# Pair transposes, sums from the pair's sum, a ScalarE read for a drain, and a new order of all queues, in a gated linear attention with a maxout layer behind it

## Chip, cores, metric

One core of a Trainium2 chip. The metric is the device time of one execution in microseconds (us), as the median of several runs. All text below says TensorE (PE, weight loads PEld), VectorE (DVE), ScalarE (ACT), GpSimd (POOL) and SyncE (SP).

## The reference

```python
# q, k, v, f_logit: (4, 8, 768, 48) float32
f = 1.0 / (1.0 + np.exp(-f_logit))
for t in range(S):
    state = f[:, :, t, :, None] * state + np.einsum('bhd,bhe->bhde', k[:, :, t], v[:, :, t])
    y[:, :, t] = np.einsum('bhd,bhde->bhe', q[:, :, t], state)
x = y.transpose(0, 2, 1, 3).reshape(B * S, H * D)      # 3072 x 384
out = np.maximum(x @ w1, x @ w2) @ w_out               # d_ff 1024
```

The kernel cuts the sequence into chunks and works through 12 steps (three windows of 256 positions for each of four batches). It uses max(a, b) = relu(a - b) + b: with wd = w1 - w2 and m2 = w2 w_out, the layer is relu(x wd) w_out + x m2.

## The kernel before

A list of words sets the order in which instructions enter each engine's queue; a number behind a letter is the step. The words that matter here: E (exponential and logarithm), C (sums over positions, on TensorE), X (exponentials of the sums), K and Q (scaled k and q), V (cast of v), T (transposes), A (scores), S (part of y that comes from the state), Y (part of y from the values, then y to SBUF), D and N (state update), d (h pieces), o (o pieces), and w words for the weights. These parts are touched (cut; `...` marks cuts):

```python
def stage_E(s):                                   # ScalarE
    nc.scalar.activation(flat(tmp), flat(loaded[s]["f"]), AF.Exp, bias=0.0, scale=-1.0)
    nc.scalar.activation(pad("ell", s)[:, :, :, 0:D], by_parity(tmp), AF.Ln, bias=1.0, scale=1.0)

def stage_C(s):                                   # 4 matmuls of 384 columns, 8 of 2
    ...
    for pt in range(2):
        for par in range(2):
            nc.tensor.matmul(out=..., lhsT=u_str if par > pt else u_inc,
                             rhs=ell[:, par, :, 0:D], start=(par == 0), stop=(par == 1))
    for j in range(NP):
        for par in range(2):
            nc.tensor.matmul(out=..., lhsT=ell[:, par, 2*j:2*j+2, :]..., rhs=ones2, ...)

def stage_T(s):                                   # 64 transposes in 64x64 tiles
    for x, nm in enumerate(("kp", "qp")):
        for j in range(NP):
            for par in range(2):
                for r in range(2):
                    for h in range(2):
                        nc.tensor.transpose(out=ps[h][r*DP:(r+1)*DP, x, j, par, :],
                            in_=src[rows, par, 2*j + r, :], identity=ident[rows, rows])

def stage_Yv(s):
    mark()                                        # nc.tensor.drain().then_inc(s_sem, 1)
    nc.tensor.wait_ge(s_sem, s_tick[s])           # S has to be in PSUM before Y adds to it
    for j ... for par ... for r ... for h in range(2):
        nc.tensor.matmul(out=ys[s][h]..., lhsT=vb[...], rhs=m[...], ...)
```

## Time and profile before

| | before |
|---|---|
| time, median of the first runs | 165.42 us (165.03 to 168.61) |
| span of the profiled execution (167.49 us) | 165.6 us |
| first h piece starts (end of the start) | 38.95 us |
| first h piece to the start of the last o piece's second part ("the middle") | 121.1 us |
| TensorE instructions | 5564 |

The two rows on the start and the middle come from TensorE's timeline. This profile is of a slow execution: 167.49 us, 2 us above the median here. So differences of start and middle to it can be too large by as much; the times and ratios are the measure.

### The profile page before, as it was taken

The page shows a single profiled execution, that of the slowest core. Times are in us where ns is not written, and L with a number is a line of the kernel's source. Part 1 is how long each engine was busy: PE and PEld are TensorE (multiplying, and loading weights), DVE is VectorE, ACT ScalarE, POOL GpSimd, SP SyncE. Part 2 cuts the span into 40 slices and gives each one's busy share as a digit, 9 for nine tenths or more (in the row PEclk, how much of TensorE's full clock was granted, in tenths as well). Part 3 has the DMA queues.
Part 4 walks back from the last instruction along what each step waited for, and adds up shares of the span by engine and source line. Part 5 has one row for each costly group of instructions (what it writes and reads, how often), then busy time and mean ns, then how long its engine had stood idle before and what let it go on. Part 6 is the DMA issues. An engine that isn't in the chain of part 4 may idle for free.

```text
span 165.6 us, 6262 instructions
## 1 busy us (share of the span) xinstructions
PE 137.5 (83%) x2780; PEld 97.4 (59%) x2781; DVE 102.8 (62%) x178; ACT 86.4 (52%) x166; POOL 46.0 (28%) x51
## 2 busy tenths in 40 slices
PE   0339839999999689999479998979985999999990
PEld 0226725557867466866347666757754776778650
DVE  6947799658659949898507729576979136201121
ACT  3568325479994966959222962717122723454400
POOL 7341611040633504390000985115410001000000
PEclk9999985899999999999978999999999999999999
DMA  5999999999999999985968096100153002202004
GB/s 137 261 304 358 331 337 363 231 276 262 265 252 258 242 272 260 299 236 144 275 177 192 4 251 194 50 16 0 53 155 113 4 0 105 101 16 95 4 22 168
DMA packets 55132, 29.32 MB, mean 177 GB/s; under 512 B 50624, under 2 KB 52800, under 8 KB 55104
## 3 DMA queue, kind: packets, MB, share of 16 engines
q1 hardware_dynamic: 53568, 28.32, 65.9%
q10 hardware_dynamic: 1536, 0.59, 1.5%
q8 instruction: 22, 0.36, 1.0%
q14 instruction: 6, 0.05, 0.1%
HBM read 23.59 MB, written 4.72 MB: 171 GB/s over the span
## 4 chain that ended last, share of the span: by engine, by line
PEld 34%; issue 21%; PE 12%; DMA 12%; PEldq 5%; SPq 5%; DVE 4%; POOL 3%; ACT 1%; ACTq 1%; POOLq 0%; DVEq 0%
PEld L363 12%; PEld L376 6%; DMA xT<-xT 6%; DMA kt<-in_k_dram 5%; PEldq L270 5%; PE o L376 5%; SPq L92 4%; PEld L232 3%; PE h L363 3%; PEld L249 3%; PEld L309 2%; PEld L373 2%; PE o L373 2%; PE y L309 2%; POOL qp L215 2%
## 5 line engine op out<-in xcount | busy, mean ns | idle before, releaser
L365 ACT ACTIVATE gT<-h 128x512 bf16<-128x512 f32 x48 | 27.7, 607 | 31.3 <-PE h L363 27.7
L363 PE MATMUL h<-xT,wd 128*128 128x256 bf16 x288 | 35.4, 273 | 5.3 <-issue 3.3
L376 PE MATMUL o<-wo,gT 128*128 128x384 bf16 x192 | 36.4, 335 | 0.3 <-issue 0.3
L378 DVE COPY ob<-o 128x384 f32<-128x384 f32 x24 | 13.2, 553 | 36.9 <-PE o L376 36.8
L261 DVE TENSOR_TENSOR at_m<-at,mask 128x512 bf16<-128x512 f32 x48 | 29.8, 681 | 5.8 <-PE at L249 5.8
L363 PEld LDWEIGHTS <-wd 128*128 128x128 bf16 x288 | 27.0, 98 | 10.0 <-issue 5.7
L340 POOL TENSOR_TENSOR state<-tmp_s,f_last 128x256 bf16<-128x256 f32 x16 | 11.6, 730 | 61.1 <-DVE tmp_s L339 55.4
L376 PEld LDWEIGHTS <-gT 128*128 128x128 bf16 x192 | 19.1, 100 | 13.8 <-issue 1.9
L215 POOL TENSOR_TENSOR kp<-kt,f_inv 128x768 bf16<-128x768 f32 x9 | 16.3, 1814 | 25.0 <-ACT f_inv L208 19.9
L347 ACT CAST xT<-y 128x512 bf16<-128x512 f32 x24 | 12.9, 588 | 12.7 <-PE y L309 12.5
L236 DVE COPY trs<-trp 128x1024 bf16<-128x1024 bf16 x24 | 15.4, 683 | 2.2 <-PE trp L232 1.8
L190 PE MATMUL cum<-ell,u_inc 128*128 128x384 bf16 x36 | 10.8, 358 | 6.3 <-ACT ell L181 6.2
L373 PE MATMUL o<-m,xT 128*128 128x384 bf16 x72 | 15.9, 330 | 0.0
L208 ACT ACTIVATE f_inv<-cum 128x384 f32<-128x384 f32 x24 | 10.4, 487 | 8.0 <-PE cum L197 5.6
L180 ACT ACTIVATE tmp_e<-ft 128x768 f32<-128x768 f32 x12 | 10.4, 868 | 4.8 <-DMA ft<-in_f_logit_dram 3.0
L249 PE MATMUL at<-trs 48*64 48x128 bf16 x384 | 9.6, 236 | 3.3 <-DVE trs L236 2.0
L215 POOL TENSOR_TENSOR qp<-qt,f_dec 128x768 bf16<-128x768 f32 x6 | 11.9, 1986 | 0.0
L219 DVE CAST vb<-vt 128x768 bf16<-128x768 f32 x12 | 11.2, 933 | 1.0 <-DMA vt<-in_v_dram 1.0
L208 ACT ACTIVATE f_dec<-cum 128x384 f32<-128x384 f32 x24 | 10.6, 505 | 0.0
L309 PE MATMUL y<-at_m,vb 64*64 64x128 bf16 x384 | 8.9, 226 | 1.7 <-PEq L270 0.6
L181 ACT ACTIVATE ell<-tmp_e 128x768 bf16<-128x768 f32 x12 | 10.1, 843 | 0.4
L249 PEld LDWEIGHTS <-trs 48*64 48x64 bf16 x384 | 7.2, 118 | 5.3 <-issue 2.8
(60 smaller groups left out, 149.3 us busy)
## 6 DMA issues: line engine op xcount, KB each, us to landing
ft<-in_f_logit_dram SPq DMA_DIRECT2D x12, 384.0 KB, 6.3
vt<-in_v_dram SPq DMA_DIRECT2D x12, 384.0 KB, 6.4
kt<-in_k_dram SPq DMA_DIRECT2D x12, 384.0 KB, 6.3
qt<-in_q_dram SPq DMA_DIRECT2D x12, 384.0 KB, 6.2
out_dram<-ob SPq DMA_DIRECT2D x12, 384.0 KB, 3.1
w_f<-in_moe_w_dram SPq DMA_DIRECT2D x6, 512.0 KB, 7.4
wo_f<-in_moe_w_out_dram SPq DMA_DIRECT2D x2, 768.0 KB, 9.4
xT<-xT ACTq DMA_DIRECT2D x24, 24.0 KB, 3.4
```

What stands on the lines that cost most here:

```text
L208: nc.scalar.activation(t[:, pt, :], ps[pt][:, 0:HD], AF.Exp, bias=0.0, scale=scale)
L215: engine.tensor_mul(pad(nm + "p", s)[:, :, :, 0:D], by_parity(loaded[s][nm]), t.rearrange("p two (h d) -> p two h d", h=H))
L236: nc.vector.tensor_copy(t[:, h], ps[h])
L249: nc.tensor.matmul(out=ps[r][h * HC:(h + 1) * HC, j % 2, par, :], lhsT=t[rows, h, 0, j, par, :], rhs=t[rows, h, 1, j].rearrange("p a t -> ...
L261: nc.vector.tensor_mul(m[:, r, 2 * jj:2 * jj + 2], ps[r], mask.rearrange("p j a b t -> p j a (b t)"))
L309: nc.tensor.matmul(out=ys[s][h][r * DP:(r + 1) * DP, j, :], lhsT=vb[rows, par, 2 * j + r, :], rhs=m[rows, r, j, par, :], start=first, stop ...
L347: nc.scalar.copy(x[:, :, :, h, :], ps.rearrange("p j (a t) -> p j a t", a=2))
L363: nc.tensor.matmul(out=ps[:, f, :], lhsT=wd[:, kt, ff * C:(ff + 1) * C], rhs=xT[g][:, kt, :], start=(kt == 0), stop=(kt == KT - 1))
L365: nc.scalar.activation(gT[g][:, 2 * fp:2 * fp + 2, :], ps, AF.Relu)
L373: nc.tensor.matmul(out=ps, lhsT=xT[g][:, kt, cols], rhs=m2[:, kt, :], start=(kt == 0), stop=False)
L376: nc.tensor.matmul(out=ps, lhsT=gT[g][:, ff, cols], rhs=wo[:, ff, :], start=False, stop=(ff == FG - 1))
L378: nc.vector.tensor_copy(obs[g][:, par, :], ps)
```

## The change

Intent: fewer TensorE instructions (transposes by pairs, sums of both positions of a pair formed beforehand), no drain of TensorE between S and Y, and a new order of every queue to fit. The new list does more than reorder: among other things it moves three scalings of k and two of the three weight subtractions from VectorE to GpSimd, two casts of wd from ScalarE to VectorE and one cast of v from VectorE to ScalarE, and it loads the weights part by part. "The new order" below means all of this. Core of the diff (abridged; order lists, the removed lines of stage C and helpers for single weight parts left out):

```diff
 def stage_E(s):
-    nc.scalar.activation(pad("ell", s)[:, :, :, 0:D], by_parity(tmp), AF.Ln, bias=1.0, scale=1.0)
+    nc.scalar.activation(flat(both), flat(both), AF.Ln, bias=1.0, scale=1.0)
+    nc.scalar.copy(even, both[:, :, 0, :])
+def stage_e(s, engine):                       # GpSimd for words e, VectorE for words g
+    engine.tensor_add(pad("es", s)[:, :, 0:D], both[:, :, 0, :], both[:, :, 1, :])
 def stage_C(s):
+    nc.tensor.matmul(out=outs[0], lhsT=ident, rhs=even, start=True, stop=False)
+    nc.tensor.matmul(out=outs[0], lhsT=u_str, rhs=es[:, :, 0:D], start=False, stop=True)
+    nc.tensor.matmul(out=outs[1], lhsT=u_inc, rhs=es[:, :, 0:D], start=True, stop=True)
+    for j in range(NP): nc.tensor.matmul(out=..., lhsT=es[:, 2*j:2*j+2, :]..., rhs=ones2, ...)
 def stage_T(s):
-    for r in range(2):
-        for h in range(2):
-            nc.tensor.transpose(out=ps[h][r*DP:(r+1)*DP, x, j, par, :], in_=src[rows, par, 2*j+r, :], ...)
+    for h in range(2):
+        pair = src[rows, par, 2*j:2*j+2, :].rearrange("p r d -> p (r d)")
+        nc.tensor.transpose(out=ps[h][:, x, j, par, :], in_=pair, identity=ident[rows, rows])
+def stage_Z(s):                               # placed by its own word in the order
+    nc.scalar.copy(seen, ys[s][1][:, :, 0])   # Y's first matmul into this bank waits for the read
 def stage_Yv(s):
-    mark()
-    nc.tensor.wait_ge(s_sem, s_tick[s])
-    ... for h in range(2):
+    ... for h in (1, 0):
```

More of the change, by code (lines that the diff above doesn't have):

```diff
@@ L17 @@
 ORDER = """
-P Lf:0 Lv:0 Lf:1 Lk:0 Lq:0 E0 V0 C0 Lq:1 X0 W2 q0 E1 K0 Lk:1 Lv:1 T0 C1 Wo wca0 wcp2 D0 A0 Lf:2 N0
-W1 X1 Lf:3 S0 k1 V1 Lk:2 Lf:4 wca1 Y0 Lq:2 wT0 wT1 Q1 wT2 wop1 woa0 Lv:2 D1 Lk:3 woa3 T1 E2 N1 wov2
-Lv:3 Lv:4 A1 S1 wm0 wm2 Lq:3 ws0 Y1 ws1 Lf:5 C2 wm1 ws2 wd11v Lv:5 X2 wd00v wm5 Lq:4 wm4 Lq:5 E3 wm3
-Lk:4 wd10v Lf:6 wd02a wd12v Lf:7 wd01a Lk:5 C3 K2 Lf:8 Lv:6 q2 X3 V2 d0.0 T2 D2 E4 d0.1 d0.2 d0.3 V3
-Lf:9 Lk:6 N2 d1.0 d1.1 A2 d1.2 d1.3 K3 C4 o0.0 Q3 T3 X4 Lq:6 S2 V4 E5 Y2 D3 N3 A3 Lq:7 C5 Lk:7 Lk:8
@@ L23 @@
-q4 o0.1 X5 o1.0 K4 E7 T4 Lf:10 Lv:7 E6 d2.0 Lq:8 S3 Y3 A4 q5 V5 C6 o1.1 X6 Lk:9 d2.1 Lk:10 K5 K6 T5
-C7 X7 d2.2 d2.3 E8 D4 q6 D5 Lq:9 d3.0 Q7 V6 N4 N5 d3.1 d3.2 k7 S4 Y4 A5 o2.0 Lv:8 C8 E9 V7 X8 d3.3
-o2.1 T7 Lk:11 S5 Y5 T6 d4.0 d4.1 Lq:10 o3.0 A6 D6 d4.2 K8 Q8 N6 d4.3 V8 Lf:11 C9 o3.1 X9 E11 S6 E10
-D7 Y6 o4.0 d5.0 N7 Lv:9 K9 Lv:10 o4.1 A7 T8 Q9 d5.1 C11 V9 X11 d5.2 d5.3 d6.0 D8 T9 S7 Y7 Lq:11 D9
-A8 k11 o5.0 d6.1 C10 X10 q10 d6.2 V10 K10 d6.3 o5.1 d7.0 Q11 o6.0 T10 Lv:11 S8 Y8 D10 A9 V11 o6.1 S9
@@ L28 @@
-Y9 A10 T11 d7.1 d7.2 d7.3 d8.0 d8.1 o7.0 d8.2 o7.1 d8.3 A11 S10 D11 Y10 d9.0 o8.0 o8.1 d9.1 d9.2
-d9.3 S11 Y11 d10.0 d10.1 o9.0 o9.1 d10.2 d10.3 d11.0 d11.1 d11.2 d11.3 o10.0 o11.0 o11.1 o10.1
+Lf:0 W2:2 E0 Lk:0 wca2 W2:0 P Lf:1 e0 Lv:0 wca0 Lq:0 C0 Wo:0 X0 K0 E1 V0 wT0 D0 Lf:2 g1 N0 wov1 W2:1
+Wo:1 E2 q0 Lk:1 T0 wcp1 C1 g2 Lq:1 Lv:1 X1 woa3 A0 S0 W1:1 Z0 Lf:3 wT1 C2 W1:2 wov0 K1 X2 W1:0 Lk:2
+q1 wT2 wop2 Y0 T1 Lq:2 V1 wm0 E3 wsp1 Lf:4 A1 wm1 D1 Lv:2 wsp2 K2 wm2 g3 S1 Lq:3 Lf:5 Q2 wsv0 N1
+Lk:3 C3 Z1 Lv:3 X3 Y1 E4 wd02v Q3 wd00v wd01v Lq:4 wd12v wd10v Lk:4 Lf:6 wd11v T2 Lv:4 Lk:5 d0.0 e4
@@ new lines @@
+d0.1 d0.2 V2 Lf:7 A2 D2 K3 Lq:5 Lv:5 E5 d0.3 wm5 wm3 d1.0 d1.1 N2 wm4 d1.2 C4 S2 V3 Z2 Lf:8 X4 Q4 T3
+D3 Lv:6 g5 N3 Lq:6 Y2 d1.3 A3 C5 V4 K4 X5 o0.0 E6 o0.1 D4 Lf:9 S3 Z3 T4 Lq:7 Lk:6 Lv:7 N4 q5 Lf:10
+E7 Y3 d2.0 g7 o1.0 A4 d2.1 K5 Lk:7 d2.2 e6 Lk:8 C7 Lq:8 Lv:8 T5 X7 C6 Lf:11 X6 E8 V5 e8 o1.1 A5 Q6
+S4 Z4 d2.3 d3.0 D5 Y4 d3.1 Lq:9 N5 V6 o2.0 K6 Lk:9 S5 Z5 E9 o2.1 e9 Y5 T6 K7 d3.2 d3.3 d4.0 d4.1 q7
+A6 Lv:9 Lv:10 C8 X8 K8 d4.2 d4.3 C9 Lk:10 X9 T7 D6 V8 V7 N6 E11 o3.0 e11 q8 E10 o3.1 o4.0 e10 D8 D7
@@ L30 @@
+S6 N7 A7 Z6 Y6 o4.1 d5.0 V9 d5.1 d5.2 d5.3 S7 T8 Z7 K9 Y7 d6.0 Q9 C11 X11 d6.1 Lq:10 o5.0 d6.2 Lk:11
+d6.3 T9 A8 S8 Lq:11 Z8 o5.1 V10 Lv:11 d7.0 o6.0 Y8 D9 o6.1 K11 d7.1 A9 C10 Q11 X10 S9 Z9 q10 d7.2
+d7.3 d8.0 K10 Y9 T10 o7.0 D10 A10 d8.1 o7.1 U11 d8.2 d8.3 S10 T11 Z10 Y10 D11 o8.0 o8.1 d9.0 A11 S11
+d9.1 d9.2 Z11 d9.3 d10.0 d10.1 Y11 o9.0 d10.2 d10.3 o9.1 o10.0 d11.0 d11.1 d11.2 d11.3 o10.1 o11.0
+o11.1
 """
@@ L97, with load_rows, load_wo @@
     wo_f = wst.tile([C, FG, HD], F32, name="wo_f")
-    def load_rows(dst, w):
-        for kt in range(KT):
-            nc.sync.dma_start(out=dst[:, kt, :], in_=w[kt * C:(kt + 1) * C, :])
-    def load_wo():
-        for h in range(2):
-            part = slice(h * FG // 2, (h + 1) * FG // 2)
-            nc.sync.dma_start(out=wo_f[:, part, :],
-                              in_=moe_w_out.rearrange("(j p) m -> p j m", p=C)[:, part, :])
+    def load_rows(dst, w, kt):
+        nc.sync.dma_start(out=dst[:, kt, :], in_=w[kt * C:(kt + 1) * C, :])
+    def load_wo(h):
+        part = slice(h * FG // 2, (h + 1) * FG // 2)
+        nc.sync.dma_start(out=wo_f[:, part, :],
+                          in_=moe_w_out.rearrange("(j p) m -> p j m", p=C)[:, part, :])
     tri = consts.tile([C, 2, HC], BF16, name="tri")
@@ L127 @@
     padded = {}
-    for nm, n_bufs in (("ell", 2), ("kp", 3), ("qp", 2), ("vb", 3)):
+    for nm, n_bufs in (("es", 2), ("kp", 3), ("qp", 2), ("vb", 3)):
         padded[nm] = []
         for i in range(n_bufs):
-            t = consts.tile([C, 2, H, DP], BF16, name=f"{nm}{i}")
+            t = consts.tile([C, H, DP] if nm == "es" else [C, 2, H, DP], BF16, name=f"{nm}{i}")
             nc.vector.memset(t, 0.0)
@@ L176, in by_parity @@
         return t.rearrange("p h two d -> p two h d")
+    ell = {}
     def stage_E(s):
-        tmp = work.tile([C, H, 2, D], F32, name="tmp_e", tag="tmp_e", bufs=1)
-        nc.scalar.activation(flat(tmp), flat(loaded[s]["f"]), AF.Exp, bias=0.0, scale=-1.0)
-        nc.scalar.activation(pad("ell", s)[:, :, :, 0:D], by_parity(tmp), AF.Ln, bias=1.0,
-                             scale=1.0)
-    def stage_C(s):
-        ell = pad("ell", s)
-        cum[s] = []
-        for pt in range(2):
-            ps = bank("cum")
-            for par in range(2):
-                nc.tensor.matmul(out=ps[:, 0:HD].rearrange("p (h d) -> p h d", h=H),
-                                 lhsT=u_str if par > pt else u_inc, rhs=ell[:, par, :, 0:D],
-                                 start=(par == 0), stop=(par == 1))
-            cum[s].append(ps)
-        ps = cum[s][0]
+        both = work.tile([C, H, 2, D], F32, name="both", tag="both")
+        even = work.tile([C, H, D], BF16, name="even", tag="even")
+        nc.scalar.activation(flat(both), flat(loaded[s]["f"]), AF.Exp, bias=0.0, scale=-1.0)
+        nc.scalar.activation(flat(both), flat(both), AF.Ln, bias=1.0, scale=1.0)
+        nc.scalar.copy(even, both[:, :, 0, :])
+        ell[s] = (both, even)
@@ new lines, in stage_e @@
+    def stage_e(s, engine):
+        both = ell[s][0]
+        engine.tensor_add(pad("es", s)[:, :, 0:D], both[:, :, 0, :], both[:, :, 1, :])
+    def stage_C(s):
+        even, es = ell.pop(s)[1], pad("es", s)
+        cum[s] = [bank("cum") for _ in range(2)]
+        outs = [ps[:, 0:HD].rearrange("p (h d) -> p h d", h=H) for ps in cum[s]]
+        nc.tensor.matmul(out=outs[0], lhsT=ident, rhs=even, start=True, stop=False)
+        nc.tensor.matmul(out=outs[0], lhsT=u_str, rhs=es[:, :, 0:D], start=False, stop=True)
+        nc.tensor.matmul(out=outs[1], lhsT=u_inc, rhs=es[:, :, 0:D], start=True, stop=True)
@@ L195, in stage_C @@
         for j in range(NP):
-            for par in range(2):
-                nc.tensor.matmul(out=ps[:, HD + 2 * j:HD + 2 * j + 2],
-                                 lhsT=ell[:, par, 2 * j:2 * j + 2, :].rearrange("p h e -> p (h e)"),
-                                 rhs=ones2, start=(par == 0), stop=(par == 1))
+            nc.tensor.matmul(out=cum[s][0][:, HD + 2 * j:HD + 2 * j + 2],
+                             lhsT=es[:, 2 * j:2 * j + 2, :].rearrange("p h e -> p (h e)"),
+                             rhs=ones2, start=True, stop=True)
@@ L216, in stage_M, with stage_V @@
                           t.rearrange("p two (h d) -> p two h d", h=H))
-    def stage_V(s):
-        nc.vector.tensor_copy(pad("vb", s)[:, :, :, 0:D], by_parity(loaded[s]["v"]))
+    def stage_V(s, copy):
+        copy(pad("vb", s)[:, :, :, 0:D], by_parity(loaded[s]["v"]))
     def stage_T(s):
@@ L228, in stage_T @@
                 for par in range(2):
-                    for r in range(2):
-                        for h in range(2):
-                            rows = slice(h * HC, (h + 1) * HC)
-                            nc.tensor.transpose(out=ps[h][r * DP:(r + 1) * DP, x, j, par, :],
-                                                in_=src[rows, par, 2 * j + r, :],
-                                                identity=ident[rows, rows])
+                    for h in range(2):
+                        rows = slice(h * HC, (h + 1) * HC)
+                        pair = src[rows, par, 2 * j:2 * j + 2, :].rearrange("p r d -> p (r d)")
+                        nc.tensor.transpose(out=ps[h][:, x, j, par, :], in_=pair,
+                                            identity=ident[rows, rows])
         for h in range(2):
@@ L249, in stage_A @@
                             nc.tensor.matmul(out=ps[r][h * HC:(h + 1) * HC, j % 2, par, :],
-                                             lhsT=t[rows, h, 0, j, par, :],
-                                             rhs=t[rows, h, 1, j].rearrange("p a t -> p (a t)"),
-                                             start=True, stop=True, skip_group_check=True)
+                                                  lhsT=t[rows, h, 0, j, par, :],
+                                                  rhs=t[rows, h, 1, j].rearrange("p a t -> p (a t)"),
+                                                  start=True, stop=True, skip_group_check=True)
             at[s, jj] = ps
@@ L262, in stage_A_dve @@
                                      mask.rearrange("p j a b t -> p j a (b t)"))
-    ys, s_tick, s_open = {}, {}, []
-    s_sem = tc.alloc_semaphore("s_done")
-    def mark():
-        if s_open:
-            nc.tensor.drain().then_inc(s_sem, 1)
-            s_tick[s_open.pop()] = len(s_tick) + 1
+    ys = {}
     def has_state(s, h):
@@ L293, in stage_S @@
                         start=(j == 0), stop=False, skip_group_check=True)
-                    s_open[:] = [s]
+    def stage_Z(s):
+        seen = work.tile([C, NP], F32, name="seen", tag="seen")
+        nc.scalar.copy(seen, ys[s][1][:, :, 0])
     def stage_Yv(s):
         m, vb = at.pop(s), pad("vb", s)
-        mark()
-        if s in s_tick:
-            nc.tensor.wait_ge(s_sem, s_tick[s])
         for j in range(NP):
@@ L305, in stage_Yv @@
                 for r in range(2):
-                    for h in range(2):
+                    for h in (1, 0):
                         rows = slice(h * HC, (h + 1) * HC)
@@ L363, in piece_d @@
                 nc.tensor.matmul(out=ps[:, f, :], lhsT=wd[:, kt, ff * C:(ff + 1) * C],
-                                 rhs=xT[g][:, kt, :], start=(kt == 0), stop=(kt == KT - 1))
+                                      rhs=xT[g][:, kt, :], start=(kt == 0), stop=(kt == KT - 1))
         nc.scalar.activation(gT[g][:, 2 * fp:2 * fp + 2, :], ps, AF.Relu)
@@ L373, in piece_o @@
             nc.tensor.matmul(out=ps, lhsT=xT[g][:, kt, cols], rhs=m2[:, kt, :],
-                             start=(kt == 0), stop=False)
+                                  start=(kt == 0), stop=False)
         for ff in range(FG):
@@ L417, with subtract @@
     wdn = []
-    def subtract(kt):
+    def subtract(kt, engine):
         if not wdn:
             wdn.append(wst.tile([C, KT, d_ff], BF16, name="wdn", tag="w_b"))
-        nc.vector.tensor_sub(wdn[0][:, kt, :], w1_f[:, kt, :], w2_f[:, kt, :])
+        engine.tensor_sub(wdn[0][:, kt, :], w1_f[:, kt, :], w2_f[:, kt, :])
     def wd_permuted(h, i, copy):
@@ L436, in rows_of @@
     def rows_of(dst, w):
-        return lambda a: load_rows(dst, w)
+        return lambda a: load_rows(dst, w, int(a))
     steps = {
@@ L441 @@
         "Lq": lambda a: load("q", int(a)), "Lv": lambda a: load("v", int(a)),
-        "W1": rows_of(w1_f, moe_w1), "W2": rows_of(w2_f, moe_w2), "Wo": lambda a: load_wo(),
-        "E": attention(stage_E), "C": attention(stage_C), "X": attention(stage_X),
+        "W1": rows_of(w1_f, moe_w1), "W2": rows_of(w2_f, moe_w2), "Wo": attention(load_wo),
+        "E": attention(stage_E), "e": lambda a: stage_e(int(a), nc.gpsimd),
+        "g": lambda a: stage_e(int(a), nc.vector), "C": attention(stage_C), "X": attention(stage_X),
         "K": lambda a: stage_M(int(a), "k", nc.gpsimd), "k": lambda a: stage_M(int(a), "k", nc.vector),
         "Q": lambda a: stage_M(int(a), "q", nc.gpsimd), "q": lambda a: stage_M(int(a), "q", nc.vector),
-        "V": attention(stage_V), "T": attention(stage_T), "S": attention(stage_S),
+        "V": lambda a: stage_V(int(a), nc.vector.tensor_copy), "U": lambda a: stage_V(int(a), nc.scalar.copy),
+        "T": attention(stage_T), "S": attention(stage_S), "Z": attention(stage_Z),
         "A": lambda a: (stage_A(int(a)), stage_A_dve(int(a))),
@@ L455 @@
         "wm": lambda a: m2_natural(int(a)) if int(a) < KT else m2_permuted(int(a) - KT),
-        "ws": attention(subtract), "wd": lambda a: wd_permuted(int(a[0]), int(a[1]), copies[a[2]]),
+        "ws": lambda a: subtract(int(a[1]), nc.vector if a[0] == "v" else nc.gpsimd), "wd": lambda a: wd_permuted(int(a[0]), int(a[1]), copies[a[2]]),
     }
```

## The prediction

> **What bounds the kernel now.** I read the busy shares first, then the slices, the chain of waits, and last TensorE's own timeline, because the first three do not say why TensorE loses time. From the page:
>
> ```profile
> span 165.6 us, 6262 instructions
> PE 137.5 (83%) x2780; PEld 97.4 (59%) x2781; DVE 102.8 (62%) x178; ACT 86.4 (52%) x166; POOL 46.0 (28%) x51
> PE   0339839999999689999479998979985999999990
> PEclk9999985899999999999978999999999999999999
> PEld 34%; issue 21%; PE 12%; DMA 12%; PEldq 5%; SPq 5%; DVE 4%; POOL 3%; ACT 1%; ACTq 1%; POOLq 0%; DVEq 0%
> q8 instruction: 22, 0.36, 1.0%
> ```
>
> TensorE (PE with PEld) is the only engine near full, and the chain is TensorE's for most of its length; but 21% of it is "issue", a wait for nothing that the profile shows. To see how much of the busy time is work, I took each stage's pace from distances between starts at full clock: 64 transposes of one step (T) 0.55 us; sums and logarithms' totals (C) 0.86 us, from 0.163 us for each of four 384-column matmuls and 0.026 for each of eight 2-column ones; scores (A) 0.45; state part of y (S) 0.22; value part (Y) 0.47; state update (D) 0.29; an h piece 0.65; an o piece 1.79. All stages of all steps come to some 118 us of the 165.6. The rest is lost in three places: about 21 us before the first h piece at 38.95 us, about 21 us between there and 145.4, and 4 us after the last matmul. The timeline of TensorE shows two of the losses in the middle:
>
> ```profile
> 70.51 0.63 PE L290 MATMUL y<-trs,state 48*64 48x128 bf16 x16
> 71.23 0.64 PE L309 MATMUL y<-at_m,vb 64*64 64x128 bf16 x32
> 71.70 0.62 PE L249 MATMUL at<-trs 48*64 48x128 bf16 x32
> ...
> 79.82 0.72 PE L363 MATMUL h<-xT,wd 128*128 128x256 bf16 x5
> 83.84 0.94 PE L363 MATMUL h<-xT,wd 128*128 128x256 bf16 x7 [3.30 <-issue]
> ...
> 125.41 0.25 PE L232 MATMUL trp<-ident,qp 64*64 64x64 bf16 x7
> 127.21 0.38 PE L232 MATMUL trp<-ident,qp 64*64 64x64 bf16 x25 [1.55 <-issue]
> ```
>
> The reader is to see, first, that Y starts 0.72 us after S though S needs 0.22: that is the drain. Second, that TensorE stops in the middle of a group, with nothing to wait for: 3.30 us at 80 (3.5 beyond pace), 1.23 at 107, 0.33 at 121, 1.55 at 125.7. Counted in the instruction order, these stops lie 1020, 510 and 254 instructions apart, all close to multiples of 255. The table by stretches shows what follows the first stop:
>
> ```profile
> 0.00:39.00 39.00, 25.66 (x453) 16.80 (x455) 29.82 (x62) 20.89 (x37) 13.47 (x25) 0.91 1.09 287
> 80.00:88.00 8.00, 4.70 (x27) 2.38 (x25) 1.24 (x2) 1.63 (x3) 0.00 (x0) 0.81 0.81 200
> 88.00:145.40 57.40, 52.68 (x1154) 38.78 (x1153) 36.35 (x58) 26.23 (x51) 16.55 (x14) 1.00 0.31 88
> ```
>
> The granted clock (third column from the end) fell to 0.81 in 80 to 88, and one o piece there took 1.5 us more. The first 39 us are bound by transfers (DMA share 1.09, 287 GB/s) and by the chain of weight products.
>
> [...] 22 instruction packets for 0.36 MB are 16 KB each, near TensorE's 5564 instructions at 64 bytes; and the stops lie on such boundaries. [...] The trace shows about 0.10 us from the end of a stream to the first matmul of the other tile size (h at 63.54 to T at 64.29, A at 59.96 to C at 60.53). [...] The eight 2-column matmuls with 128-column weights start 26 ns apart, so the load there is fast; no run here shows it for a 64-row tile. [...]
>
> **The change part by part.** *Sums.* Four 384-column matmuls become three and eight small ones four: 3 x 0.163 + 4 x 0.026 = 0.59 us instead of 0.86, so 12 x 0.27 = 3.2 us off TensorE. For it ScalarE gets a copy of 128x384 a step (0.50 us by the like rows of f_dec and f_inv), and VectorE or GpSimd an addition (about half of their 128x768 products). *Drain.* S to Y loses 0.50 us where Y follows at once (0.72 less 0.22); in 10 steps that are not hidden, 5.0 us. In its place ScalarE reads four columns of y (0.21 us, by the 128x8 row) and Y waits for that; in the new order TensorE has between S and Y at least 0.45 us of other work (step 6), mostly 0.6 to 4 us. I count 1.0 us in all for waits that show. *Transposes.* 64 in four tiles at 8.5 ns become 32 in two tiles. A tile streams 64 columns (27 ns) and now loads 128; if the load hides as elsewhere, some 16 to 18 ns each, if half does, 22. I choose 22: 0.70 us a step instead of 0.55, 12 x 0.15 = 1.8 us more. *Tile modes.* 64x128 is a mode of its own: counted in the orders of both kernels, changes of mode go from 42 to 76, 34 x 0.10 = 3.4 us more. *Instruction fetch.* 5564 TensorE instructions become 4676. More important, I added the paces over each stretch of 255: before, the stretches ahead of the four stops hold 1.87, 1.42, 2.01 and 2.79 us of work; afterwards the shortest stretch holds 4.75. As a stretch that lasts over 3.5 us never had a stop at its end, I expect none: 3.30 + 1.23 + 0.33 + 1.55 = 6.4 us, and 1.5 us of low clock after the first. *Start.* Weight loads are spread: the last part of w_out now has 5.5 MB ahead of or in it instead of 6.3, at 287 GB/s 2.8 us earlier, so the m2 products start earlier; the last of w1 comes 0.35 MB (1.2 us) later. The first h piece should start near 36 instead of 38.95: 3 us off. *ScalarE crowding* (12 x 0.71 = 8.5 us more work): 1.0 us.
>
> The sum: -3.2 - 5.0 + 1.0 + 1.8 + 3.4 - 7.9 - 3.0 + 1.0 = -11.9 us of span, 153.7 instead of 165.6. The profiled execution took 167.49 us for a span of 165.6, 1.9 more; so 155.6, which I call 155.5.
>
> **The rivals.** *Slow pair loads.* If a 128-column load into a 64-row tile is not hidden, T costs what the w2 transposes cost in kind: they ran 95 ns apart (24 from 18.14 us on) where streaming needs 53. [...] Against it: 256- and 384-column matmuls hide their loads wholly. *Stops only in the profiled run.* The profiled execution took 167.49 us, the fastest timed one 165.03: part of the 7.9 us may be special to it. With none of it to win, the timed median 165.42 less 4 gives 161. For the stops in every run: they follow the program's order. *ScalarE takes over.* Its work grows from 86.4 to about 95 us; between 39 and 80 us it was already busy 31.9 of 41. [...] the new read stands in that queue ahead of relus and exponentials; each microsecond that a read waits for S would delay h banks. That would make 158 to 160. Against it: its load stays below TensorE's in every stretch. *The start stays transfer-bound.* Then the 3 us do not come: 158.5.
>
> **Range and chances.** The gains from sums and drain (8.2) are nearly sure, the fetch gain likely, and the losses I added (7.2) are partly guesses, too high if the pair transposes run at full pace and if mode changes overlap. Both good together give 151.5; two rivals together give 161. Faster by over 2% means below 162.1; only slow pair loads of over 1.5 us a step, or all rivals at once, miss that: 0.92, 0.07 for the same, 0.01 slower.
>
> **What would show it.** Right: no "issue" idle above 0.5 us on TensorE after the first h piece, no granted clock under 0.95 there, 18 or 19 instruction packets; Y's waits for the ScalarE read below 0.3 us each; 32 transposes in 0.55 to 0.85 us; C in 0.6; first h piece before 37; after it TensorE busy above 90%. The prediction is wrong if stops inside groups remain with longer stretches (then they are not fetches), if 32 transposes take over 1 us, if the wait for the ScalarE read becomes a large row among the waits, or if changes of mode cost over 0.2 us each.

## More of the kernel before

Most of the lines of this profile are in the prediction. Three more, from its list of waits (who waited for whom: us in total, times, longest):

```profile
PE h L363 <- issue: 3.3, 1, 3.3
PEld L309 <- PEq L270: 2.7, 10, 0.5
PE h L363 <- DMA xT<-xT: 1.6, 1, 1.6
```

The first is a stop that has no cause in the profile; the second is the drain (L270), short each time; the third is a wait for the small copy that moves part of x to other partitions.

## The result

The changed kernel takes 156.2 us in the median (154.61 to 157.2, 4 runs), the kernel before 165.9 in the same rounds. The ratio is 0.940, 95% interval 0.929 to 0.951. (Ratios here are the mean time of one kernel's runs over that of the other's of the same rounds, so not quite the ratio of the medians quoted.) Executions over 1.5% slower than the fastest of the same kernel are left out of the means. The forecast was 155.5, with 151.5 to 161 as the range.

The page of the changed kernel, the same lines as before:

```profile
span 155.4 us, 5393 instructions
PE 130.6 (84%) x2337; PEld 92.4 (59%) x2337; DVE 105.0 (68%) x180; ACT 91.6 (59%) x188; POOL 64.0 (41%) x63
PE   0243595997889699999999969999999999999990
PEclk9999998699999999999999999999999999999999
PE 61%; DVE 19%; DMA 8%; SPq 5%; issue 3%; ACT 1%; DVEq 0%; ACTq 0%
q8 instruction: 18, 0.29, 0.8%
```

"Issue" has gone from 21% of the chain to 3%, TensorE itself carries 61%, and the low clock in the middle is gone. (This profile, too, is of its kernel's slowest execution, 157.2 us.) The first ten digits of TensorE's row are as poor as before. Its timeline, the stages that answer to those of the kernel before:

```profile
53.03 0.32 PE L200 MATMUL cum<-even,ident 128*128 128x384 bf16 x1 [1.30 <-DVE tmp_s L339]
...
67.65 0.62 PE L289 MATMUL y<-trs,state 48*64 48x128 bf16 x16
68.20 1.48 PE L363 MATMUL h<-xT,wd 128*128 128x256 bf16 x12
69.62 0.45 PE L323 MATMUL sadd<-vb,kp 64*64 64x64 bf16 x32
69.89 0.62 PE L309 MATMUL y<-at_m,vb 64*64 64x128 bf16 x32
...
91.56 0.75 PE L255 MATMUL at<-trs 48*64 48x128 bf16 x16 [1.31 <-DVE ob L378]
...
97.76 0.41 PE L239 MATMUL trp<-ident,kp 64*128 64x64 bf16 x16
98.00 0.40 PE L239 MATMUL trp<-ident,qp 64*128 64x64 bf16 x16
98.33 0.64 PE L309 MATMUL y<-at_m,vb 64*64 64x128 bf16 x32
```

No group is broken by "issue" any more. Between S (67.65) and Y (69.89) TensorE does h pieces and D, so Y waits for nothing. The 32 pair transposes take 0.57 us from 97.76 to 98.33, with one change of tile size in it. Waits for VectorE of 1.30 and 1.31 us are new. The stretches (start and length, busy times and counts, then granted clock, DMA share, GB/s):

```profile
0.00:39.00 39.00, 22.44 (x362) 13.86 (x362) 31.49 (x61) 22.97 (x46) 22.17 (x29) 0.96 1.03 277
80.00:88.00 8.00, 8.00 (x119) 5.55 (x119) 7.13 (x13) 7.74 (x19) 4.14 (x4) 1.00 0.74 178
88.00:135.00 47.00, 45.38 (x884) 33.59 (x883) 29.46 (x48) 22.29 (x49) 14.36 (x13) 1.00 0.44 128
```

From 80 to 88 us TensorE is busy for all 8.00 us where it had been for 4.70. The start is no shorter: the first h piece comes at 39.59 instead of 38.95. So the whole gain lies in the middle, 110.3 us instead of 121.1. And it is not less work on TensorE: adding up the paces of all stages and 0.10 us for each change of tile size gives about 124 us for both kernels (an estimate of mine, from the paces), since the 3.1 us saved in C go into the extra changes of size: 76 instead of 42, and 62 with the new order alone. The VectorE timeline of the start and of the wait at 53 us shows why these are slow:

```profile
27.85 2.48 DVE L226 CAST vb<-vt 128x768 bf16<-128x768 f32 x1
...
33.45 2.83 DVE L422 TENSOR_TENSOR wdn<-w_f 128x1024 bf16<-128x1024 f32 x1
...
50.68 1.96 DVE L192 TENSOR_TENSOR es<-both 128x384 bf16<-128x384 f32 x1
```

The same three kinds of instruction took 0.55, 1.22 and 0.54 us where GpSimd was idle or nearly so; here GpSimd ran a product or a subtraction beside them.

### The profile page after: what moved, and what is told of

Its sections match the earlier page's. It is cut to its first block, busy times and chain, and to the rows that moved or that the text cites. A ratio compares the mean times of both kernels' runs of the same rounds, so it can differ in the third digit from the quotient of the medians.

```text
span 155.4 us, 5393 instructions
## 1 busy us (share of the span) xinstructions
PE 130.6 (84%) x2337; PEld 92.4 (59%) x2337; DVE 105.0 (68%) x180; ACT 91.6 (59%) x188; POOL 64.0 (41%) x63
## 4 chain that ended last, share of the span: by engine, by line
PE 61%; DVE 19%; DMA 8%; SPq 5%; issue 3%; ACT 1%; DVEq 0%; ACTq 0%
PE h L363 18%; PE o L376 18%; PE o L373 7%; DMA wo_f<-in_moe_w_out_dram 4%; SPq L94 4%; PE trp L239 4%; DMA out_dram<-ob 4%; PE at L255 3%; DVE vb L226 3%; DVE qp L222 3%; PE y L309 3%; DVE at_m L267 3%; DVE trs L242 3%; PE y L289 2%; DVE wd L428 2%
## 5 line engine op out<-in xcount | busy, mean ns | idle before, releaser
L376 PE MATMUL o<-wo,gT 128*128 128x384 bf16 x192 | 35.1, 326 | 0.0
L340 POOL TENSOR_TENSOR state<-tmp_s,f_last 128x256 bf16<-128x256 f32 x16 | 10.9, 686 | 38.0 <-DVE tmp_s L339 38.0
L222 POOL TENSOR_TENSOR kp<-kt,f_inv 128x768 bf16<-128x768 f32 x12 | 22.2, 1852 | 10.3 <-ACT f_inv L215 6.8
L184 ACT ACTIVATE both<-ft 128x768 f32<-128x768 f32 x12 | 10.4, 869 | 7.9 <-DMA ft<-in_f_logit_dram 6.3
L226 DVE CAST vb<-vt 128x768 bf16<-128x768 f32 x11 | 11.8, 1077 | 4.2 <-DMA vt<-in_v_dram 4.2
L222 POOL TENSOR_TENSOR qp<-qt,f_dec 128x768 bf16<-128x768 f32 x6 | 11.9, 1977 | 5.0 <-ACT even L186 2.5
L200 PE MATMUL cum<-even,ident 128*128 128x384 bf16 x12 | 4.5, 374 | 8.2 <-ACT even L186 6.9
L185 ACT ACTIVATE both<-both 128x768 f32<-128x768 f32 x12 | 10.1, 843 | 0.4
L255 PE MATMUL at<-trs 48*64 48x128 bf16 x384 | 9.1, 229 | 1.4 <-DVE ob L378 1.3
L192 POOL TENSOR_TENSOR es<-both 128x384 bf16<-128x384 f32 x7 | 8.0, 1146 | 5.5 <-ACT both L185 5.5
L255 PEld LDWEIGHTS <-trs 48*64 48x64 bf16 x384 | 6.7, 113 | 4.2 <-issue 3.8
```

Of the source, the lines that this page charges most:

```text
L222: engine.tensor_mul(pad(nm + "p", s)[:, :, :, 0:D], by_parity(loaded[s][nm]), t.rearrange("p two (h d) -> p two h d", h=H))
L226: copy(pad("vb", s)[:, :, :, 0:D], by_parity(loaded[s]["v"]))
L255: nc.tensor.matmul(out=ps[r][h * HC:(h + 1) * HC, j % 2, par, :], lhsT=t[rows, h, 0, j, par, :], rhs=t[rows, h, 1, j].rearrange("p a t -> ...
L376: nc.tensor.matmul(out=ps, lhsT=gT[g][:, ff, cols], rhs=wo[:, ff, :], start=False, stop=(ff == FG - 1))
```

## The experiments

Theory 1: TensorE stopped at boundaries of 256 instructions because the next packet of its program had not come (in the profile before, 22 packets of 16 KB, 0.36 MB, carry its 5564 instructions); fewer instructions and an order without dense stretches remove the stops. Theory 2: less work (sums), a cheaper hand-over (read for drain) and faster transposes make the gain. Theory 3: the order alone makes it. In the table, "start" is the first h piece and "middle" runs from there to the start of the last o piece's second part, both in the profiled execution.

| run | what it is | median us | ratio to before (95%) | start | middle |
|---|---|---|---|---|---|
| before | | 164.7 to 166.9 | 1 | 38.95 | 121.1 |
| changed | | 156.2 | 0.940 (0.929 to 0.951) | 39.59 | 110.3 |
| b_shift | before + 80 useless matmuls first | 161.84 | 0.982 (0.975 to 0.989) | 38.60 | 116.4 |
| b_pair | before + pair transposes | 159.0 | 0.965 (0.961 to 0.970) | 35.88 | 115.8 |
| b_sums | before + new sums | 175.49 | 1.070 (1.060 to 1.079) | 38.26 | 130.1 |
| b_read | before + read for drain | 168.32 | 1.021 (1.015 to 1.027) | 40.15 | 120.6 |
| a_order_only | new order, old operations | 157.13 | 0.944 (0.935 to 0.954) | 38.49 | 112.3 |
| a_oldT | changed, old transposes | 155.03 | 0.934 (0.924 to 0.943) | 38.42 | 109.0 |
| a_drain | changed, drain for read | 157.02 | 0.942 (0.928 to 0.955) | 39.32 | 110.2 |
| a_oldsums | changed, old sums | 154.09 | 0.920 (0.906 to 0.934) | 38.69 | 109.0 |
| a_order_shift | a_order_only + 40 useless matmuls | 159.62 | 0.975 (0.961 to 0.989) | 38.43 | 113.4 |
| a_allpool | changed, all additions on GpSimd | 158.59 | 0.966 (0.952 to 0.979) | 42.96 | 108.6 |
| a_best | a_oldsums, start relieved | 155.39 | 0.947 (0.934 to 0.960) | 37.78 | 109.8 |
| a_best2 | a_best, old transposes, 40 useless matmuls | 158.53 | 0.968 (0.955 to 0.981) | 38.95 | 112.3 |

The rows from b_shift to b_read ran together, as did the next four and the last four; the kernel before had medians of 164.71, 166.9 and 166.38 there, so differences of a per cent between groups mean little. The ratio of a_oldsums rests on two runs of four, and those of the last group on two runs of the kernel before.

**b_shift: more work, other boundaries.**

```diff
 def stage_C(s):
+    if s == 0:
+        idle = bank("idle")
+        for _ in range(80):
+            nc.tensor.matmul(out=idle[:, 0:2], lhsT=u_inc, rhs=ones2, start=True, stop=True)
```

> The kernel before with 80 useless two-column matmuls put ahead of everything on TensorE, while it waits for the first data; they move every later boundary of 256 instructions by 160. Theory 1 (TensorE stops where a stretch of 256 instructions holds less than about 3.5 us of work, because its next 16 KB of instructions are not there yet): the work in the stretches after the start that fall short of 3.5 us was 2.4, 2.2, 1.6, 2.3 and 3.1 us, together 5.9 us short; after the move only 1.7 and 3.3 remain short, 2.0 us together. The stops at 80, 107, 121 and 126 us go, one of 1 to 2 us may come near 53 us, and the time falls by 3 to 6 us (160 to 163) although work was added. Theory 2 (the stops have another cause, such as waits that the profile does not show, or belong to the stage): the stops stay in the same stages, the time stays within 1 us or grows by up to 2.

160.15 to 162.48 us, 1.8% less with 160 instructions more. TensorE's timeline of this run, at the stages where the kernel before stopped for 3.30 us:

```profile
78.59 1.49 PE L367 MATMUL h<-xT,wd 128*128 128x256 bf16 x12
...
81.79 0.63 PE L253 MATMUL at<-trs 48*64 48x128 bf16 x30
82.94 0.24 PE L253 MATMUL at<-trs 48*64 48x128 bf16 x2 [0.51 <-issue]
```

The twelve h matmuls that had been torn after the fifth run through. The stop has moved to two matmuls before the end of A in step 6, which is instruction 3090 (of loads and matmuls, the 160 useless ones not counted); the boundary worked out from the old stops lies at 3089. The small one near 50 us (0.21 us) is at 1562, worked out 1559. So the stops belong to places in the instruction stream and not to stages. The work between boundaries explains less: the stretch ahead of 3089 was not among those that I had called short.

The count can be made sharper than I made it. When every TensorE instruction of the trace is counted, drains and semaphore instructions too, the four stops of the kernel before follow 3009, 4033, 4545 and 4800 instructions, and those of this run 1729 and 3266. Each number is a multiple of 256 plus 192 to 194, and so is that of every stop by "issue" after the first h piece in the other runs. The "multiples of 255" are multiples of 256 of which some instructions were not counted.

In this run the granted clock also fell to 0.50 for 3.4 us at 120.4 us, after an idle time of 1.34 us in a wait for VectorE; this takes back part of the gain in this execution, and it shows that a low clock can come without a long stop.

**b_pair: only the pair transposes, in the old order** (the diff of stage_T above).

> The kernel before with only the pair transposes (32 in 64x128 tiles instead of 64 in 64x64). Work on TensorE stays the same: 0.49 us a step instead of 0.54, with some 6 more changes of tile size at 0.1 us. Theory 1 (instruction fetch): 768 instructions fewer, and no stretch of 255 after the start holds less than 4.0 us, so all stops go: 5 to 8 us less, 158 to 161. Theory 2 (only work and waits count): within 1 us of the time before.

158.68 to 159.04 in three of its four runs. Its timeline shows no idle time of 0.3 us or more by "issue" on TensorE after the first h piece; its instruction packets are 19 instead of 22. The transposes take 0.49 us without the change of size, at 15.3 ns each, against 0.54 before; that accounts for 0.6 of the 5.7 us. Its start is also 3 us earlier: its granted clock stays at 1.00 from 20 to 40 us, where the kernel before ran m2 products at 0.50 from 23.5 to 30.3. Its middle is 5.3 us shorter, though the waits for the copy of x grow from 1.6 to 3.4 us. The stops have gone, as Theory 1 has it, and Theory 2 fails. How much of the timed 5.7 us is the stops and how much the clock at the start stays open.

**b_sums and b_read: the other two operations in the old order.**

```diff
 # b_sums: stages E, e and C as in the change; in the old order
-... C2 ...
+... g2 C2 ...        # g (VectorE) in steps 1, 2, 3, 5, 7; e (GpSimd) in the others
 # b_read: Z as in the change, no drain; in the old order
-... S2 Y2 ...
+... S2 Z2 Y2 ...
```

> The kernel before with only the sums taken from the sum of each pair (C: 0.86 to 0.60 us), the addition placed right ahead of C in the old order, on VectorE in steps 1, 2, 3, 5 and 7, else on GpSimd. Theory 2 (work): 3.1 us less on TensorE, some of it lost to the longer way from the logarithm to C and to ScalarE's copies: 163 to 165. Theory 1 (fetch): 120 instructions fewer also move the boundaries; by chance no stretch after the start then holds less than 3.6 us, so the stops go too and it comes to 157 to 160.

> The kernel before with only the ScalarE read of y in place of the drain, right between S and Y as the old order has them. Both theories: the instruction count stays and so do the stops. What it tells is the cost of the hand-over by itself: a drain cost 0.72 - 0.45 = 0.27 us a step; the way over ScalarE (end of S, read of 0.21 us, back to TensorE) should take 0.5 to 0.7 us where ScalarE is free and more where it is not, so 12 steps are 3 to 6 us slower than before, 168 to 172.

The sums alone lose 10.8 us, a miss by 10 or more. The waits of this run say where:

```profile
PE cum L202 <- DVE es L193: 8.3, 5, 3.3
PE cum L202 <- POOL es L193: 7.5, 3, 6.0
```

TensorE waits 15.8 us for the additions, which stand in queues behind other work: the work saved is 3.1 us, the longer way costs five times that. Around the two longest of these waits the granted clock also fell to 0.50, for 6.8 us each time. The stops did not all go either: one of 0.83 us is left near 91 us. The read alone loses 3.6 us in the median, as both theories had it:

```profile
PE y L304 <- ACT seen L292: 8.6, 11, 3.5
```

Eleven waits of 0.8 us in the mean for a read of 0.2 us, where the drain cost about 0.27. In the changed kernel this row is absent. The stops near 80 and 107 us stay in the same groups, as expected, at 0.59 and 0.90 us; those near 121 and 126 us are not in this profile. The longest wait, 3.54 us, is followed by 3.4 us at a clock of 0.50. So two of the three operations are losses until the order hides their ways.

**a_order_only: the new order with none of the operations** (words e, g and Z taken out of it).

> The new order of all queues with the old operations: 64x64 transposes, sums from all halves, drain. It tells what the order alone is worth. Work on TensorE with changes of tile size comes to 125.9 us against 123.5 in the changed kernel, the drains add some 2 us, and with 5564 instructions two stretches of 255 hold only 2.3 and 1.9 us, which stop TensorE for about 1 us each if instruction fetch is the cause. 156.2 + 2.4 + 2 + 2: 161 to 165, so less than half of the gain. If the order is what counts, as most of the waits would say, it lies within 2 us of the changed kernel, 156 to 158.

156.62 to 158.09 us, ratio 0.944 against 0.940 for the whole change. My expectation of 161 to 165 was wrong; Theory 3 is nearly all of it, within intervals of about 1% either way (1.6 us). Of the two stops of about 1 us that I expected, the one behind the stretch of 2.3 us did not come. The other did, at instruction 3504, exactly on the boundary worked out beforehand, behind the stretch that I had counted at 1.9 us of work (a small one of 0.30 us came near 48 us):

```profile
90.20 0.64 PE L307 MATMUL y<-at_m,vb 64*64 64x128 bf16 x31 [0.15 <-PEq L268]
92.17 0.24 PE L307 MATMUL y<-at_m,vb 64*64 64x128 bf16 x1 [1.32 <-issue]
```

The middle is 8.8 us shorter than before. Of that the profiles name 4.8 us of stops (6.4 before, 1.32 and 0.30 now), 1.5 us of low clock behind the long stop, 1.6 us of waiting for the copy of x, and about 1.3 us of waits for VectorE (0.44, 0.41 and 0.50 us). All of these are things that an order changes. No run separates the sequence from the moves of work between engines that come with it, so which of the two brings the gain is not shown.

**a_oldT, a_drain, a_oldsums: one operation taken back in the changed kernel.**

```diff
 # a_oldT:    stage_T of before
 # a_drain:   mark() and wait_ge of before in stage_Yv, words Z taken out
 # a_oldsums: stages E and C of before, words e and g taken out
```

> The changed kernel with the old transposes, 64 in 64x64 tiles (5444 TensorE instructions instead of 4676). Fetch theory: one stretch after the start holds only 1.8 us (ending in step 3 or so) and two more 3.4 and 3.7, so one or two stops of about 1 us come back near 55 us; there are 12 to 24 fewer changes of tile size, 1 to 2 us less. Sum: 155.5 to 158, so the pair transposes are worth at most 2 us once the order keeps the stretches long, against 5.7 us in the old order. Rival (the pair transposes are faster in themselves): 3 us or more slower than the changed kernel, 159 or more.

> The changed kernel with the drain ahead of Y in place of the ScalarE read. In the new order TensorE has other work between S and Y, so the drain only empties the array once more per step: about 0.2 to 0.3 us, 12 times, 2.4 to 3.6 us: 158 to 160. My prediction's 0.50 us a step would give 161 to 162. If the read is hidden no better than a drain, 155.5 to 156.5.

> The changed kernel with the old sums (four 384-column and eight two-column matmuls, no addition and no copy). TensorE gets 12 x 0.27 = 3.2 us more work, and one stretch of 255 holds only 1.8 us, so a stop of about 1 us; ScalarE and GpSimd have 6 and 8 us less. If TensorE's work sets the time: 159 to 161. If the longer way through copy and addition costs as much as it saves, 155 to 157.

The three stand at 155.03, 157.02 and 154.09 us. The drain comes out like the read (intervals overlap; middle 110.2 and 110.3). The old transposes are no slower; the stops that came back are of 0.30 and 0.46 us only. The old sums are, if anything, faster than the new ones; the intervals of the two, from different groups of runs, just overlap. C does take 2.1 us less in the middle of the changed kernel (5.0 instead of 7.1 by the sums of that timeline), but the stage A, with the waits that follow it, takes 9.7 instead of 5.7: the three waits for VectorE near 43, 53 and 91 us are not in the run with the old sums. The stop of about 1 us that I expected behind a stretch of 1.8 us is not there either: by the trace that stretch lasted 2.4 us and TensorE went through.

**a_order_shift: the boundaries moved in the new order.**

```diff
 # a_order_only with
+        for _ in range(40):
+            nc.tensor.matmul(out=idle[:, 0:2], lhsT=u_inc, rhs=ones2, start=True, stop=True)
```

> The new order with the old operations again, and 40 useless two-column matmuls ahead of everything, which move the boundaries of 256 instructions by 80. In the run without them one stretch held 1.9 us and TensorE stopped for 1.32 us at its end, on the last matmul of Y in step 6, as counted; after the move no stretch is more than 0.8 us short of 3.9. Fetch theory: that stop goes and nothing over 0.5 us takes its place, 155 to 156.5 (ratio to the kernel before about 0.935 after 0.944), so the order alone equals the whole change. Rival: the stop stays at Y of step 6, 157 to 158.

159.14 to 160.32 us: not faster; by the ratio slower, but that compares two groups, and the middle is only 1.1 us longer than in a_order_only. From its TensorE timeline:

```profile
50.78 0.32 PE L200 MATMUL cum<-ones,ell 128*128 128x2 bf16 x7
52.39 0.18 PE L200 MATMUL cum<-ones,ell 128*128 128x2 bf16 x1 [1.30 <-issue]
...
84.09 0.39 PE L325 MATMUL sadd<-vb,kp 64*64 64x64 bf16 x25
85.31 0.25 PE L325 MATMUL sadd<-vb,kp 64*64 64x64 bf16 x7 [0.83 <-issue]
```

The stop in Y of step 6 is gone, as expected. But two others came, one of 1.30 us in C of step 5 at instruction 1722, and one of 0.83 us inside D of step 6 at 3250 (and one of 0.63 us in Y at 57.9 us, which the profile puts down to ScalarE, lies on a boundary too); worked out were boundaries at 1719 and 3249. So the place was right again and the threshold wrong: the stretch ahead of 3249 held 4.0 us of work by my count. The record of the instruction packets shows why a fixed threshold fails: the packet started some 2.4 us after TensorE had entered the stretch before. For the four stops of the kernel before that was 3.2, 0.7, 0.7 and 3.2 us. The DMA share was 0.99 in those 2.4 us and 0.08 where 0.7 us passed, but also 0.53 in one case of 3.2 us, so that the data transfers delay the packets is a guess. Five stretches of only 1.8 to 2.6 us (in b_shift, a_oldT, a_oldsums, a_best and a_order_only) ended with a stop of 0.30 us or none; there the packet had started as TensorE entered them, or up to 0.5 us before. TensorE went on 1.35 to 1.6 us after the packet had landed, in all eight stops whose times I compared; and at none of the 271 boundaries in the 14 traces did it go on sooner than 1.26 us after the landing (packets and boundaries matched in their order).

**a_allpool: additions off VectorE** (words g made e).

> The changed kernel with all twelve additions of the sums on GpSimd, none on VectorE. If what the sums saved on TensorE is lost in waits for VectorE, which is crowded near 50 and 90 us (an addition of 0.55 us took 1.96 us there, and TensorE waited 1.30 us for the sums): those waits shrink, 1 to 2 us less than the changed kernel, 153.5 to 155.5. If it is the added work beside GpSimd that slows VectorE, or GpSimd's own queue that delays the sums, no gain or a loss: 156 to 159.

Both halves came true at once. The middle is the shortest of all, 108.6 us, and the wait at 91 us is gone. The wait for the sums at 53 us is not: it comes at 56 us, 1.24 us long, now for GpSimd. And the start is 3.4 us longer, because an addition now waits in GpSimd's queue behind the subtractions of weights; TensorE then ran at a clock of 0.50 from 37.1 to 40.5 us:

```profile
36.57 0.32 PE L201 MATMUL cum<-es,u_str 128*128 128x384 bf16 x1 [3.06 <-POOL es L192]
...
56.27 0.32 PE L201 MATMUL cum<-es,u_str 128*128 128x384 bf16 x1 [1.24 <-POOL es L192]
```

**a_best and a_best2: towards a faster version.**

```diff
 # a_best: a_oldsums with
-wsp1 ... wsp2 ... wd12v wd10v ... wd11v
+wsv1 ... wsv2 ... wd12a wd10a ... wd11a     # subtractions to VectorE, three evacuations to ScalarE
 # a_best2: a_best with the old transposes and 40 useless matmuls first
```

> The changed kernel with the old sums, as in the run that came to 154.1 us, and with the start relieved: the two subtractions w1 - w2 from GpSimd (2.35 us each, beside which VectorE's casts took 2.48 us instead of 0.55) to VectorE (1.22 us), and three of the six evacuations of wd from VectorE to ScalarE. If the start is bound by VectorE, slowed by GpSimd, the first h piece comes 1.5 to 3 us earlier than 38.7 and the time is 151.5 to 153. If the start is bound by transfers (the last part of w1 comes near 31 us), it stays near 154.

> The same relieved start and old sums, with the old 64x64 transposes too and 40 useless matmuls ahead of everything, so that no stretch of 255 instructions holds less than 3.3 us; the ScalarE read stays. Of the change there remain the order and the read. If pair transposes and sums give nothing once the order is right and the stretches are long: the same as the run with pair transposes, 151.5 to 153.5, perhaps 1 us less for some 30 fewer changes of tile size. If the pair transposes are worth something: 1 to 3 us more than that run.

The relieved start brings the first h piece to 37.78 us, 0.9 us earlier, less than expected, and the time (154.81 to 155.70 in three runs, 160.3 in one) is not below that of a_oldsums. a_best2 has two stops in the middle, 1.45 us in Y of step 3 and 1.21 in D of step 6, and is 3 us slower than a_best, as if the pair transposes were worth 3 us here: with 848 instructions more (80 of them the useless ones) stretches end in stops again, although by my count none held less than 3.3 us; by the trace the two ahead of these stops lasted 4.9 and 4.0 us. No version here is clearly faster than the changed kernel; a_oldsums, with 154.09 and the ratio 0.920, is the candidate. A mixed form, additions on VectorE in the first steps and on GpSimd later, was not run.

## Why the prediction was right, and where its steps failed

The time (155.5 forecast, 156.2 measured) and the main mechanism held; several terms of the sum were wrong and cancelled. That the time came so close is partly luck: the sum of -11.9 was taken off the slow execution of 167.49 us, and off the median of 165.42 it would have given 153.5. The profiled spans fell by 10.2 us, all of it in the middle, where 8.9 had been forecast.

- **Instruction fetch, -7.9.** Right in cause: b_shift, b_pair and a_order_shift moved or removed the stops to the instruction. Right in effect: the changed kernel has none, and 18 packets. Its size is smaller: b_pair, without stops, gained 5.7 us and b_shift, with small ones, 3.0 (5.3 and 4.7 in the middle of the profiles, against the slow profile of before). The prediction's test of "over 3.5 us never had a stop" was too sharp: in its own trace the stretch ahead of the stop at 125.7 us had lasted 4.2 us, waits included, and in a_best2 one of 4.9 us ended in a stop of 1.45. The changed kernel's shortest stretch after the start lasted 5.6 us, and none stopped it. The low clock at the start of the kernel before, 0.50 from 23.5 to 30.3 us, came with short idle times: TensorE's longest from 20 to 25 us were 1.2 and 1.7 us.
- **Drain, -5.0, and read, +1.0.** The failed step is "S needs 0.22". The 16 matmuls of S start 27 ns apart and take 0.45 us; so a drain cost 0.27 us, not 0.50. In the new order it costs nothing that can be seen: a_drain equals the changed kernel. The read is indeed hidden.
- **Sums, -3.2.** C fell to 0.60 us as worked out, but the path did not get the gain: it came back as waits for VectorE (a_oldsums, a_allpool). The prediction booked 1.0 us for ScalarE and nothing for VectorE or GpSimd; this is the term that was missing.
- **Transposes, +1.8.** Mis-sized: the 22 ns each was an estimate that no trace showed; measured are 15.3 ns each, 0.49 us a step, slightly less than before. Over two tiles that is 31 ns a tile, so the load of 128 columns hardly shows beside the 27 ns that 64 columns stream (an estimate from the 0.163 us of 384 columns). **Tile modes, +3.4:** the 0.10 us a change holds (A to C, 79.32 to 79.89 us; 0.08 from 64x128 to 64x64, in the 0.57 us of the pair transposes above). Of the 34 extra changes 20 come from the new order and 14 from the pairs (a_order_only has 62). Together the two terms were booked at 5.2; a_oldT is about 1.3 us shorter in the middle than the changed kernel, which also bears its small stops.
- **Start, -3.0.** It failed: 39.59 instead of 38.95. The last part of w_out did come earlier (the last of its casts began at 24.0 instead of 25.2 us). But VectorE was slowed beside GpSimd: three of its instructions shown above lost 1.9, 1.6 and, later, 1.4 us, and TensorE waited 1.0 us at 36.3 for the second, the last subtraction of weights. a_best, which takes the subtractions off GpSimd, recovers 0.9 us; what holds the rest is not shown.
- **The order.** The prediction gave it only the fetch and the start. a_order_only shows that it is worth nearly the whole 9.7 us, and that the three operations together add nothing measurable to it in this kernel. In the sum the operations come to -1.0 net (-3.2, -5.0, +1.0, +1.8, +3.4, +1.0). That is near what the runs show, but few of the terms held one by one, so it is luck.

## What to carry to other kernels

Where a busy TensorE shows stops by "issue" in the middle of a group, count instructions between them, all that the trace has of TensorE: if the distances are multiples of 256, spread small matmuls so that no 256 instructions pass in under some 6 us, or use fewer of them. In these traces that was enough (a stretch of 4.9 us still ended in a stop of 1.45 us, one of 5.9 us in one of 0.19), and not always needed. An operation that saves work on the bound engine by a longer way through others (sums, read) was a loss in the old order here and worth little in the new one: test the order alone before crediting the operations. Before putting two-input work on GpSimd, see whether VectorE has time to be slowed: an addition of 0.54 us took 1.96 us here.
